# Strided and local attention with a dense mixture of attention experts: all weights loaded through one queue, and the planner's steps shifted by a table

## The chip, the cores and the metric

One Trainium2 chip, one of its cores. The metric is the device time of one execution in microseconds. TensorE (PE in the profile) multiplies matrices, VectorE (DVE), ScalarE (ACT) and GpSimd (POOL) work on rows of 128 partitions, SyncE (SP) issues transfers.

## The reference

Eight batches, eight heads, 576 positions, heads of 64. The first four heads see a window of 32 positions, the other four every 32nd position. The result, 512 wide, goes through four experts, each a causal attention of one head; a gate picks two experts per position.

```python
def _attn_ref(q, k, v):                      # 8, 8, 576, 64
    scores = scale * np.matmul(q, k.transpose(0, 1, 3, 2))
    mask_local = (rel >= 0) & (rel < stride)                 # stride 32
    mask_strided = (rel >= 0) & (pos[None, :] % stride == pos[:, None] % stride)
    masks = np.stack([mask_local if h < H // 2 else mask_strided for h in range(H)], axis=0)
    attn = softmax(np.where(masks, scores, -1e9))
    return np.matmul(attn, v)

def _moe_ref(x, w_gate, wq, wk, wv, wo):     # x: 8, 576, 512
    logits = x @ w_gate                      # top 2 of 4, softmax over the two
    for e in range(E):
        q, k, v = x @ wq[e], x @ wk[e], x @ wv[e]
        a = softmax(causal(scale * (q @ k.transpose(0, 2, 1))))
        ye = a @ v @ wo[e]
        out += (weight of e, where it is picked) * ye
```

## The kernel before

The kernel writes no instruction order by hand. Each step is put on a list by `op(eng, key, fn, ...)`: the engines that may run it with an assumed cost, a place on a time line (`key`), and the buffers it reads and writes. `schedule()` then plays the list through with these assumed costs: on each engine, of the steps that could start within 0.02 us of the earliest, the one with the smallest key is issued (`MODE_PEN` is added for TensorE where the shape of the rows and columns in use, the mode, would change). The order so found is the program; each engine executes its part strictly in order and waits by semaphores. A batch is `T = 52.0` wide on the time line.

`stage1(b, hp)` is the first attention of batch `b` for a pair of heads; pairs 0 and 1 are local, 2 and 3 strided. `load_qk` brings q and k into a tile `nat` (in batch 0, pairs 0 and 1 use tiles `p` of the later stage), TensorE transposes it (L422) into `qkt`, multiplies scores (L452), VectorE masks and takes maxima, GpSimd subtracts (L479), ScalarE exponentiates (L481), VectorE sums, GpSimd scales (L488), TensorE transposes the probabilities (L511, L513) into `pt` and multiplies with `v` (L537 local, L542 strided; this is called the values step). The result is kept as a sum of two reduced-precision parts, `xh` (ScalarE, L557) and `xl` (VectorE, L559). There are two tiles each of `nat`, `qkt`, `v` and `pt`, so the loads of a pair wait for the pair two before it.

`project` multiplies x with the weights of k and q (L651: 12 matmuls a group, four contraction tiles times three products of parts), `values2` those of v and the gate (L598). `attend(b, ep, ...)` does the causal attention for a pair of experts: scores (L704, L686), VectorE masks and takes the extreme (L715), ScalarE exponentiates (L722), GpSimd scales (L745, L739), TensorE transposes (L767) into `th` and multiplies with v (L803). `out_tile` multiplies with `wo` (L834) and stores.

`load_weights` brings a weight to a staging buffer and splits it, as x, into `wh` (ScalarE, L330) and `wl` (VectorE or GpSimd, L333). The staging of `wq`, `wk`, `wv` is already in the buffers `qk2` of the q and k of the second stage, that of `wo` in the buffers `ys` of the output. The load is one step for each 128 rows; `wk` and `wq` are issued by ScalarE, `wv` and `wo` by SyncE, and each waits until a given transposition of `stage1` has been issued in the planner's time line (`after=[behind]`).

Transfers of both issuing engines take eight semaphores in turn, and each waits until the transfer that last held its semaphore has landed.

## Time and profile before

| | us |
|---|---|
| median of 3 runs (lowest, highest) | 535.01 (530.88, 535.28) |
| the profiled execution | 533.24 |
| its span, first to last instruction | 531.5 |
| TensorE, VectorE, ScalarE, GpSimd busy | 500.9, 342.1, 298.7, 203.5 |

The profile is of one execution. A line number is that of the kernel; L251 is the copy out of the accumulators that all steps share. Busy time of TensorE is modelled from pipelined matmuls, so that a window that is full need not be at the engine's peak.

### The profile page before, as it was taken

The page shows a single profiled execution, that of the slowest core. Times are in us where ns is not written, and L with a number is a line of the kernel's source. Part 1 is how long each engine was busy: PE and PEld are TensorE (multiplying, and loading weights), DVE is VectorE, ACT ScalarE, POOL GpSimd, SP SyncE. Part 2 cuts the span into 40 slices and gives each one's busy share as a digit, 9 for nine tenths or more (in the row PEclk, how much of TensorE's full clock was granted, in tenths as well). Part 3 has the DMA queues.
Part 4 walks back from the last instruction along what each step waited for, and adds up shares of the span by engine and source line. Part 5 has one row for each costly group of instructions (what it writes and reads, how often), then busy time and mean ns, then how long its engine had stood idle before and what let it go on. Part 6 is the DMA issues. An engine that isn't in the chain of part 4 may idle for free.

```text
span 531.5 us, 17995 instructions
## 1 busy us (share of the span) xinstructions
PE 500.9 (94%) x7192; PEld 420.9 (79%) x7192; DVE 342.1 (64%) x1037; ACT 298.7 (56%) x829; POOL 203.5 (38%) x255
## 2 busy tenths in 40 slices
PE   4468999899999999999999999999999999999997
PEld 4458987788878887889878897789878888788864
DVE  4575488835676667865677666865778575833661
ACT  2263357743766556753666555754667555653652
POOL 6362226531544234341444243441344424520440
PEclk9965999999999999999999999999999999999999
DMA  7957333421344224541245214551245212110103
GB/s 141 175 128 160 81 87 70 107 53 24 77 118 114 58 45 109 133 100 25 61 117 130 57 29 105 140 114 26 46 130 133 47 25 65 41 42 1 41 20 100
DMA packets 138803, 43.53 MB, mean 82 GB/s; under 512 B 133856, under 2 KB 133856, under 8 KB 138720
## 3 DMA queue, kind: packets, MB, share of 16 engines
q1 hardware_dynamic: 134496, 41.34, 32.7%
q10 hardware_dynamic: 4224, 1.05, 1.0%
q8 instruction: 57, 0.93, 0.7%
q14 instruction: 26, 0.21, 0.1%
HBM read 32.92 MB, written 9.44 MB: 80 GB/s over the span
## 4 chain that ended last, share of the span: by engine, by line
PE 84%; DMA 4%; SPq 4%; DVE 3%; issue 2%; POOL 2%; ACT 1%; DVEq 0%; POOLq 0%; ACTq 0%
PE bank L651 21%; PE bank L598 11%; PE bank L834 10%; PE bank L803 9%; PE bank L704 8%; PE bank L767 6%; PE bank L452 5%; PE bank L542 4%; PE bank L537 3%; PE bank L422 3%; SPq L377 2%; DMA v<-in_v_dram 2%; PE bank L511 2%; PE bank L513 1%; SPq L371 1%
## 5 line engine op out<-in xcount | busy, mean ns | idle before, releaser
L745 POOL TENSOR_SCALAR p<-p,st,wt 128x192 f32<-128x192 f32 (+3 forms) x128 | 82.9, 662 | 69.6 <-ACT qkt L251 25.4
L722 ACT ACTIVATE p<-p,st 128x192 f32<-128x192 f32 (+3 forms) x128 | 78.3, 615 | 18.9 <-DVE st L715 18.2
L251 DVE COPY th<-bank 128x384 f32<-128x384 f32 (+2 forms) x92 | 42.4, 478 | 35.3 <-PE bank L767 30.9
L479 POOL TENSOR_TENSOR p1l<-p1l,st 128x960 f32<-128x960 f32 (+1 forms) x18 | 29.0, 1615 | 89.6 <-DVE st L477 72.9
L704 PE MATMUL bank<-qk 64*128 64x288 f32 (+3 forms) x320 | 59.2, 452 | 0.3 <-DVE pt L251 0.3
L251 ACT COPY qk<-bank 128x288 f32<-128x288 f32 x59 | 23.5, 398 | 63.2 <-PE bank L651 63.2
L715 DVE CUSTOM_DVE_ANT_0 p<-bank,m_cau 128x192 f32<-128x192 f32 (+3 forms) x128 | 57.1, 474 | 1.9 <-PE bank L704 1.4
L803 PE MATMUL bank<-th,vs 128*64 128x256 f32 (+1 forms) x512 | 57.0, 361 | 0.5 <-DVE th L251 0.4
L251 ACT COPY qkt<-bank 128x320 f32<-128x320 f32 (+3 forms) x93 | 32.9, 409 | 33.2 <-PE bank L422 24.0
L803 PEld LDWEIGHTS bank<-th,vs 128*64 128x64 f32 x512 | 35.1, 139 | 18.7 <-DVE p1s L466 1.3
L767 PEld LDWEIGHTS bank<-ident,p 64*128 64x128 f32 x896 | 38.4, 139 | 14.2 <-issue 8.0
L251 ACT COPY th<-bank 128x384 f32<-128x384 f32 (+2 forms) x100 | 40.5, 418 | 12.9 <-PE bank L767 7.4
L767 PE MATMUL bank<-ident,p 64*128 64x64 f32 x896 | 46.7, 228 | 0.2
L598 PE MATMUL bank<-wh_v,xh 128*128 128x260 f32 (+1 forms) x160 | 46.6, 291 | 0.3 <-ACT qkt L251 0.3
L488 POOL TENSOR_TENSOR p1l<-p1l,st 128x960 f32<-128x960 f32 (+1 forms) x18 | 29.0, 1614 | 46.6 <-DVE st L486 36.3
L479 POOL TENSOR_TENSOR p1s<-p1s,st 128x648 f32<-128x648 f32 (+1 forms) x18 | 20.7, 1154 | 67.3 <-DVE st L477 32.9
L598 PE MATMUL bank<-wl_v,xh 128*128 128x260 f32 (+1 forms) x160 | 45.3, 283 | 0.0
L598 PE MATMUL bank<-wh_v,xl 128*128 128x260 f32 (+1 forms) x160 | 45.0, 281 | 0.0
L452 PE MATMUL bank<-qkt 64*64 64x54 f32 (+1 forms) x1408 | 37.0, 247 | 7.2 <-ACT qkt L251 4.7
L651 PE MATMUL bank<-xh,wh_k 128*128 128x288 f32 x128 | 40.2, 314 | 0.7 <-ACT qkt L251 0.7
L452 PEld LDWEIGHTS bank<-qkt 64*64 64x64 f32 x1408 | 31.4, 144 | 11.1 <-ACT qkt L251 5.5
L559 DVE TENSOR_TENSOR xl<-bank,xh 128x320 fp32r<-128x320 f32 (+1 forms) x64 | 28.3, 454 | 18.2 <-ACT xh L557 17.9
(126 smaller groups left out, 1267.1 us busy)
## 6 DMA issues: line engine op xcount, KB each, us to landing
out_dram<-ys SPq DMA_DIRECT2D x32, 256.0 KB
v<-in_v_dram SPq DMA_DIRECT2D x32, 192.0 KB
v<-in_v_dram SPq DMA_DIRECT2D x96, 45.0 KB
nat<-in_q_dram SPq DMA_DIRECT2D x28, 144.0 KB
nat<-in_k_dram SPq DMA_DIRECT2D x28, 144.0 KB
nat<-in_q_dram SPq DMA_DIRECT2D x64, 49.5 KB
nat<-in_k_dram SPq DMA_DIRECT2D x64, 49.5 KB
nat<-in_q_dram SPq DMA_DIRECT2D x32, 45.0 KB
```

The source lines that it names most:

```text
L251: (nc.scalar.copy if e == "ACT" else nc.vector.tensor_copy)(dst, src)
L452: nc.tensor.matmul(sp[h].t[64 * hf:64 * hf + 64, nk * i:nk * i + nk], qkt.t[r, 0, q0:q0 + 64], qkt.t[r, 1, c0:c0 + nk], start=True, stop=True)
L479: nc.gpsimd.tensor_tensor(P, P, bc[0], ALU.subtract)
L598: nc.tensor.matmul(vp.t[:m, :NV], xx.t[:, t0:t0 + m], ww.t[:, kt, :], start=i == 0, stop=i == 11)
L651: nc.tensor.matmul(pj.t[:, :HS], ww.t[:, kt, ep * 128:(ep + 1) * 128], xx.t[:, c], start=i == 0, stop=i == 11)
L704: nc.tensor.matmul(sp[a].t[:, :cn], qk.t[r, 0, q0:q0 + m], qk.t[r, 1, c0:c0 + cn], start=True, stop=True)
L715: lambda e, sp=sp, p=p, a=a, c0=c0, cn=cn, hh=hh, nk=nk, acc_=acc_: nc.vector.tensor_tensor_reduce(out=p.t[:, a, c0:c0 + cn], in0=sp[a].t[ ...
L722: op({"ACT": 0.485 + 0.00083 * nk}, k_ + 1, lambda e, p=p, a=a, ci=ci: nc.scalar.activation(p.t[:, a], p.t[:, a], AF.Exp, bias=st.t[:, ci ...
L745: lambda e, p=p, a=a, ci=ci, t=t: nc.gpsimd.tensor_scalar(p.t[:, a], p.t[:, a], st.t[:, 14 + ci + a:15 + ci + a], wt.t[:, t, 2 * ep + a:2 ...
L767: nc.tensor.transpose(tp[hf].t[:, 64 * c:64 * c + 64], p2[t].t[r, a, k0:k0 + 128], ident[r, r])
L803: nc.tensor.matmul(acc.t[o, dst:dst + 128 * nb], vw, x.t[:, c:c + nb, :].rearrange("p c q -> p (c q)"), start=j == 0, stop=j == js[-1], sk ...
L834: nc.tensor.matmul(yp.t[:, :DM], xx.t[:, c0:c0 + 128], ww.t[:, ep, :], start=i == 0, stop=i == 5)
```

## The change

Three things. `load_weights` issues all weights from SyncE and no longer waits for a transposition; its places on the time line are new (`wk` 6.5 and `wq` 7.5 in place of -18 and -6.5, steps of 0.1 in place of 0.5). Every call of `op` gets a name, and a table `PRI` of 112 numbers is added to the key: one for the name, one more for the name in batch 0 and in batch 7. The planner starts VectorE, GpSimd and SyncE at 4.5, 9.0 and 0.8 in place of 0 and takes a packet of a transfer at 0.0014 in place of 0.0013. No step's function, tile or number of buffers changes.

```diff
+    batch = [0]
+
+    PRI = {
+        "acc": 1.0, "acc 0": 8.0, "acc 7": 2.0, "exp2": 1.0, "exp2 0": 10.0, "exp2 7": -4.0, "exp2_0": 15.0,
...
+        "yp_out": 18.0, "yp_out 0": -9.0, "yp_out 7": 10.0,
+    }
+
+    def op(kind, eng, key, fn, r=(), w=(), mode=None, npk=0, after=()):
...
-        o.eng, o.key, o.fn, o.mode, o.npk = eng, key, fn, mode, npk
+        o.eng, o.fn, o.mode, o.npk = eng, fn, mode, npk
+        o.key = key + PRI.get(kind, 0.0) + PRI.get(f"{kind} {batch[0]}", 0.0)
...
-        free = {e: 0.0 for e in LAT}
+        free = {"PE": 0.0, "ACT": 0.0, "DVE": 4.5, "POOL": 9.0, "SP": 0.8}
...
-                dma_free = max(dma_free, t) + o.npk * 0.0013
+                dma_free = max(dma_free, t) + o.npk * 0.0014
...
-    def load_weights(name, key, behind):
+    def load_weights(name, key):
...
-            k_ = key + 0.5 * kt
+            k_ = key + 0.1 * kt
...
-            op({"ACT" if name in "kq" else "SP": 0.55 + 0.4 * (name == "v")}, k_, load, w=[st], npk=512, after=[behind])
-            op({"ACT": act(n)}, 15 + k_ * 0.1, lambda e, kt=kt, raw=raw: nc.scalar.copy(hi.t[:, kt, :], raw()),
+            op("load_w", {"SP": 0.55 + 0.4 * (name == "v")}, k_, load, w=[st], npk=512)
+            op("hi_w", {"ACT": act(n)}, 15 + k_ * 0.1, lambda e, kt=kt, raw=raw: nc.scalar.copy(hi.t[:, kt, :], raw()),
...
-    for nm, key, hp in (("k", -18.0, 2), ("q", -6.5, 3), ("v", 12.5, 3), ("o", 14.5, 3)):
-        load_weights(nm, key, TPS[hp])
+    for nm, key in (("k", 6.5), ("q", 7.5), ("v", 12.5), ("o", 14.5)):
+        load_weights(nm, key)
```

What this does to the order is shown at three places. In the rows that follow, the numbers behind names tell buffers apart: `qkt_158` and `qkt_159` serve pairs 0 and 2, 1 and 3; `v_160` and `v_161` likewise; `nat_156` and `nat_157` serve pairs 2 and 3 in batch 0, then pairs 0 and 2, 1 and 3; `qk_143`, `qk_144`, `qk_145` stage `wk`, `wq`, `wv`. Lines of the changed kernel are 23 or 24 higher.

ScalarE in the opening, from the exponentials of pair 0 on, before:

```order
L481 ACTIVATE p1l_162<-p1l_162 128x480 x2
L251 COPY qkt_158<-bank_68 128x324
L324 DMA qk_143<-in_moe_wk_dram 128x4x64 x4
L251 COPY qkt_158<-bank_69 128x252
L251 COPY qkt_158<-bank_71 128x252
L330 CAST wh_k_222<-qk_143 128x256
```

and now:

```order
L504 ACTIVATE p1l_162<-p1l_162 128x480 x2
L275 COPY qkt_158<-bank_68 128x324
L275 COPY qkt_158<-bank_69 128x324
L275 COPY qkt_158<-bank_70 128x252
L275 COPY qkt_158<-bank_71 128x252
L504 ACTIVATE p1l_163<-p1l_163 128x480 x2
L275 COPY qkt_159<-bank_68 128x324
```

The issues of `wk` between the copies of pair 2 are gone, ScalarE makes all four copies itself, and the first cast of `wk` comes only behind pair 0's `xh`.

SyncE in the opening, from the last load of pair 1's `v` on, before:

```order
L401 DMA v_161<-in_v_dram 96x8x64
L324 DMA qk_145<-in_moe_wv_dram 128x4x64
L327 DMA qk_145<-in_moe_w_gate_dram 128x4
...
L322 DMA ys_140<-in_moe_wo_dram 128x512
L406 DMA v_160<-in_v_dram 18x10x64 x3
L409 DMA v_160<-in_v_dram 54x1x64
...
L322 DMA ys_141<-in_moe_wo_dram 128x512
L406 DMA v_161<-in_v_dram 18x10x64 x3
L409 DMA v_161<-in_v_dram 54x1x64
```

and now:

```order
L425 DMA v_161<-in_v_dram 96x8x64
L348 DMA qk_143<-in_moe_wk_dram 128x4x64 x4
L348 DMA qk_144<-in_moe_wq_dram 128x4x64
L430 DMA v_160<-in_v_dram 18x10x64 x3
L433 DMA v_160<-in_v_dram 54x1x64
...
L430 DMA v_161<-in_v_dram 18x10x64 x3
L433 DMA v_161<-in_v_dram 54x1x64
...
L348 DMA qk_144<-in_moe_wq_dram 128x4x64 x3
L348 DMA qk_145<-in_moe_wv_dram 128x4x64
L351 DMA qk_145<-in_moe_w_gate_dram 128x4
```

`wk` and a quarter of `wq` now go ahead of the `v` of pairs 2 and 3, the rest of `wq` and all of `wv` behind it.

SyncE at the loads for the strided pairs 2 and 3 of batch 2 (`nat_156`, then `nat_157`), before:

```order
L377 DMA nat_156<-in_q_dram 18x11x64 x2
L377 DMA nat_156<-in_q_dram 18x10x64
L398 DMA v_160<-in_v_dram 96x64
L401 DMA v_160<-in_v_dram 96x8x64
...
L377 DMA nat_156<-in_k_dram 18x11x64 x2
L377 DMA nat_156<-in_k_dram 18x10x64
L398 DMA v_161<-in_v_dram 96x64
```

and now:

```order
L401 DMA nat_156<-in_q_dram 18x11x64 x2
L401 DMA nat_156<-in_q_dram 18x10x64
L401 DMA nat_156<-in_k_dram 18x11x64 x2
L401 DMA nat_156<-in_k_dram 18x10x64
L422 DMA v_160<-in_v_dram 96x64
L425 DMA v_160<-in_v_dram 96x8x64
```

The `v` loads now stand behind the twelve of the tile. On TensorE the transpositions of this tile came right behind those of pair 1, one attention unit after pair 0's; now a block of 48 projection matmuls (L651) stands between the last transposition out of the buffer's earlier tile and the first out of this one.

## Rows read from the trace of the kernel before

**Rows 1.** The page: span; busy time, share and instructions of each engine; the chain that ended last by engine.

```profile
span 531.5 us, 17995 instructions
PE 500.9 (94%) x7192; PEld 420.9 (79%) x7192; DVE 342.1 (64%) x1037; ACT 298.7 (56%) x829; POOL 203.5 (38%) x255
...
PE 84%; DMA 4%; SPq 4%; DVE 3%; issue 2%; POOL 2%; ACT 1%; DVEq 0%; POOLq 0%; ACTq 0%
```

**Rows 2.** Windows: the stretch, its length, busy time and instructions of each engine in it, granted clock, share of the DMA engines, GB/s; and, from the time line of TensorE, its last matmul (start, duration).

```profile
0.00:49.04 49.04, 28.44 (x498) 25.37 (x499) 29.67 (x68) 20.41 (x52) 27.01 (x47) 0.80 0.72 147
49.04:108.08 59.04, 56.65 (x889) 48.73 (x887) 40.33 (x124) 33.42 (x98) 24.47 (x28) 0.93 0.44 96
108.08:167.19 59.11, 58.98 (x878) 49.32 (x877) 38.12 (x121) 35.92 (x100) 19.61 (x23) 1.00 0.31 76
...
470.55:531.50 60.95, 56.57 (x496) 44.21 (x495) 24.27 (x94) 27.70 (x80) 14.37 (x23) 1.00 0.12 40
...
527.41 0.40 PE L834 MATMUL bank<-wl_o,oh 128*128 128x512 f32 x1
```

**Rows 3.** Time line of ScalarE in the opening: start, duration, instruction, and in brackets the idle time before it with what ended it.

```profile
21.49 0.64 ACT L251 COPY qkt<-bank 128x252 f32<-128x252 f32 x2 [6.57 <-DMA qk<-in_moe_wk_dram]
...
29.21 0.75 ACT L251 COPY pt<-bank 96x320 f32<-96x320 f32 x2 [4.37 <-DMA qk<-in_moe_wq_dram]
```

**Rows 4.** Time line of TensorE in the opening, same columns.

```profile
21.91 1.59 PE L452 MATMUL bank<-qkt 64*64 64x54 f32 x44 [4.32 <-ACT qkt L251]
...
24.63 1.28 PE L511 MATMUL bank<-ident,p1l 64*96 64x64 f32 x20
...
29.68 2.18 PE L537 MATMUL bank<-pt,v 96*64 96x64 f32 x34 [3.37 <-ACT pt L251]
...
35.20 2.18 PE L537 MATMUL bank<-pt,v 96*64 96x64 f32 x34 [0.18 <-ACT pt L251]
...
45.32 2.64 PE L542 MATMUL bank<-pt,v 54*64 54x54 f32 x44 [1.93 <-DVE pt L251]
47.89 1.22 PE L422 MATMUL bank<-ident,nat 64*128 64x64 f32 x18
49.04 0.61 PE L651 MATMUL bank<-xh,wh_k 128*128 128x288 f32 x1
```

**Rows 5.** Time line of GpSimd in the opening, same columns.

```profile
18.57 1.93 POOL L488 TENSOR_TENSOR p1l<-p1l,st 128x480 f32<-128x480 f32 x2
...
27.17 1.42 POOL L479 TENSOR_TENSOR p1s<-p1s,st 128x324 f32<-128x324 f32 x2 [3.13 <-DVE st L477]
...
33.02 1.41 POOL L333 TENSOR_TENSOR wl_k<-qk,wh_k 128x256 fp32r<-128x256 f32 x2 [2.54 <-ACT wh_k L330]
...
36.54 1.78 POOL L488 TENSOR_TENSOR p1s<-p1s,st 128x324 f32<-128x324 f32 x2
```

**Rows 6.** Time line of SyncE's queue in the opening: the issues of `wv` with the gate, first and last, and of pair 2's `v`, first and last.

```profile
22.30 0.54 SPq L324 DMA_DIRECT2D qk<-in_moe_wv_dram  x1
...
25.96 1.61 SPq L327 DMA_DIRECT2D qk<-in_moe_w_gate_dram  x1
...
31.05 1.09 SPq L406 DMA_DIRECT2D v<-in_v_dram  x3
...
34.40 0.75 SPq L409 DMA_DIRECT2D v<-in_v_dram  x1
```

**Rows 7.** Time lines of SyncE's queue and of TensorE at two places where transpositions of q and k wait for their tile.

```profile
100.76 1.27 SPq L377 DMA_DIRECT2D nat<-in_k_dram  x3
...
221.26 1.09 SPq L377 DMA_DIRECT2D nat<-in_q_dram  x3
...
225.88 1.16 SPq L377 DMA_DIRECT2D nat<-in_k_dram  x3
...
104.68 0.85 PE L422 MATMUL bank<-ident,nat 54*128 54x54 f32 x11 [1.39 <-DMA nat<-in_k_dram]
...
229.12 0.55 PE L422 MATMUL bank<-ident,nat 54*128 54x54 f32 x11 [0.88 <-DMA v<-in_v_dram]
```

**Rows 8.** The chain that ended last, in order of time: start, duration up to the next piece, piece.

```profile
49.11 5.31 PE bank L651 x24
...
55.40 3.38 PE bank L651 x24
...
108.08 4.96 PE bank L651 x36
...
113.56 1.79 PE bank L651 x12
...
155.68 1.41 PE bank L542 x44
```

**Rows 9.** The waits of TensorE from 49 to 475 us: waiting line, what ended the wait, us in total, times, longest.

```profile
PE bank L422 <- DMA v<-in_v_dram: 1.7, 2, 0.9
PE bank L422 <- DMA nat<-in_k_dram: 1.4, 1, 1.4
...
PE bank L422 <- DMA nat<-in_q_dram: 0.2, 1, 0.2
```

**Rows 10.** Windows of the opening, columns as in the second group.

```profile
15.00:20.00 5.00, 0.46 (x4) 0.32 (x4) 2.90 (x7) 0.00 (x0) 3.33 (x4) 1.00 0.74 168
...
30.00:35.00 5.00, 5.00 (x104) 4.43 (x100) 3.01 (x7) 3.55 (x11) 1.89 (x3) 0.50 0.40 91
```

More of the change, by code (lines that the diff above doesn't have):

```diff
@@ L347, in attention_moe_kernel @@
     X = {}
-    TPS = []
     def stage1(b, hp):
+        batch[0] = b
         h0 = 2 * hp
@@ L424, in tps @@
                     c += w_
-            first = op({"PE": 0.058 * len(ws) + 0.03}, k0 - 14 + u, tps, r=[nat], w=[*tp, qkt], mode=MR)
+            op("tp", {"PE": 0.058 * len(ws) + 0.03}, k0 - 14 + u, tps, r=[nat], w=[*tp, qkt], mode=MR)
             for x in range(2):
-                op(either(cn), k0 - 13 + u, lambda e, t_=tp[x], x=x, c0=c0, cn=cn: copy(
+                op("tp_out", either(cn), k0 - 13 + u, lambda e, t_=tp[x], x=x, c0=c0, cn=cn: copy(
                     e, qkt.t[:, x, c0:c0 + cn], t_.t[:, :cn]), r=[tp[x]], w=[qkt])
         for h in range(2):
-            op({"SP": 1.0 if local else 1.9}, (k0 - 25 if b else 4.0 + hp), lambda e, h=h: load_v(e, h), w=[vt], npk=864 if local else 594)
-        TPS.append(first)
+            op("load_v", {"SP": 1.0 if local else 1.9}, (k0 - 25 if b else 4.0 + hp), lambda e, h=h: load_v(e, h), w=[vt], npk=864 if local else 594)
         sp = [RB.new(f"s{h}_{n}") for h in range(2)]
@@ L453, in scores @@
                                          qkt.t[r, 0, q0:q0 + 64], qkt.t[r, 1, c0:c0 + nk], start=True, stop=True)
-        op({"PE": 1.0 if local else 0.75}, k0 - 11, scores, r=[qkt], w=[*sp, p[0], p[1]], mode=MQ)
+        op("s", {"PE": 1.0 if local else 0.75}, k0 - 11, scores, r=[qkt], w=[*sp, p[0], p[1]], mode=MQ)
         N = 2 * ni * nk
@@ L499, in stage1 @@
                 r_, w_ = ((ph, sh), (ph + sh, ph), (ph, ph), (ph, sh), (sh, sh), (ph + sh, ph))[step]
-                op(eng, k0 - 9 + step, lambda e, step=step, h_=h_: softmax(step, h_, e), r=r_, w=w_)
+                op(f"softmax{step}", eng, k0 - 9 + step, lambda e, step=step, h_=h_: softmax(step, h_, e), r=r_, w=w_)
         ptt = PTR.new(f"pt_{n}")
@@ L521, in stage1 @@
                 rows = 96 if local else 128
-                op(either(64 * ni), k0 - 1.5 + 0.5 * u, lambda e, pt=pt, hf=hf, dst=dst, rows=rows: copy(
+                op("pt_out", either(64 * ni), k0 - 1.5 + 0.5 * u, lambda e, pt=pt, hf=hf, dst=dst, rows=rows: copy(
                     e, dst(), pt[hf].t[:rows, :64 * ni]), r=[pt[hf]], w=[ptt])
@@ L555, in xv @@
                 return t.rearrange("c (j r) -> c j r", r=STR)[:, :, c0 // NJ:(c0 + cn) // NJ]
-            op({"ACT": act(cn)}, k0 + 0.5 + 0.3 * u, lambda e, s_=sv_, xv=xv: nc.scalar.copy(xv(xh.t), s_()),
+            op("xh", {"ACT": act(cn)}, k0 + 0.5 + 0.3 * u, lambda e, s_=sv_, xv=xv: nc.scalar.copy(xv(xh.t), s_()),
                r=[xa], w=[xh[u]])
-            op({"DVE": dve(cn)}, k0 + 1 + 0.3 * u, lambda e, s_=sv_, xv=xv: nc.vector.tensor_sub(
+            op("xl", {"DVE": dve(cn)}, k0 + 1 + 0.3 * u, lambda e, s_=sv_, xv=xv: nc.vector.tensor_sub(
                 xv(xl.t), s_(), xv(f(xh.t))), r=[xa, xh[u]], w=[xl[u]])
@@ L599, in mm @@
                         i += 1
-            op({"PE": 12 * 0.121}, key + step * t, mm, r=xbufs(b) + wbufs("v"), w=[vp, vs[t]], mode=M128)
-            op(either(NV), key + step * t + 0.5, lambda e, t=t, m=m, vp=vp: copy(e, vs.t[:m, t, :], vp.t[:m, :NV]),
+            op("vp", {"PE": 12 * 0.121}, key + step * t, mm, r=xbufs(b) + wbufs("v"), w=[vp, vs[t]], mode=M128)
+            op("vp_out", either(NV), key + step * t + 0.5, lambda e, t=t, m=m, vp=vp: copy(e, vs.t[:m, t, :], vp.t[:m, :NV]),
                r=[vp], w=[vs[t]])
@@ L653, in mm @@
                         i += 1
-            op({"PE": 12 * 0.134}, key + step * u, mm, r=xbufs(b) + wbufs(nm), w=[pj, qk[j, u]], mode=M128)
-            op(either(HS), key + step * u + 0.5, lambda e, u=u, pj=pj: copy(
+            op("pj", {"PE": 12 * 0.134}, key + step * u, mm, r=xbufs(b) + wbufs(nm), w=[pj, qk[j, u]], mode=M128)
+            op("pj_out", either(HS), key + step * u + 0.5, lambda e, u=u, pj=pj: copy(
                 e, qk.t[:, j, u * HS:(u + 1) * HS], pj.t[:, :HS]), r=[pj], w=[qk[j, u]])
@@ L731, in attend @@
         kk = key + 3.6 * (len(idx) - 1) + 1.5
[L732 removed]
+        op("recip2", {"DVE": 0.4}, kk, recip, r=[st["s"]], w=[st["r"]])
         for t in idx:
@@ L858, in attention_moe_kernel @@
         k2 = T * (b + 0.75) + 3
+        batch[0] = b
         qk = [QK2.new(f"qk_{b}_{ep}") for ep in range(2)]
```

56 lines of the change are left out of this document (28 added, 28 removed), and 15 rows, old and new, of the table PRI.

## The prediction

> **What bounds the kernel now.** I read the page first: TensorE is busy 94% of the span, and the chain of work that ended last runs over it for 84% [rows 1]. Next the windows cut the span into stages, since that share is an average over stages with different limits [rows 2]. Before 49.04 us TensorE is busy for 28.44 us only; from 49.04 to 108.08 us it misses 2.39 us, in the next 59 us 0.13 us. So there are two regimes: an opening of 49 us in which TensorE waits, and some 480 us in which it is the bound and only its own work counts. The end adds little: the last window misses 4.38 us, of which 3.69 are the last copy and store behind the last matmul (527.81 us) [rows 2].
>
> The opening decides most, so I read it engine by engine. ScalarE stands still for 6.57 us in front of two copies at 21.49 us, with the four issues of `wk` ahead of them in its queue, and for 4.37 us in front of the copies at 29.21 us, behind the issues of `wq` [rows 3]. TensorE waits for exactly these copies: 4.32 us for the scores of pair 2 (21.91 us) and 3.37 us for the values step of pair 0 (29.68 us) [rows 4]. The issues take long because each waits for an earlier transfer to land; ScalarE, in program order, then cannot copy.
>
> **The change: the opening.** Three edits act together. The eight loads of `wk` and `wq` leave ScalarE for SyncE, `load_weights` no longer waits for a transposition, and the offsets in PRI rearrange what is ready. The order shows ScalarE's copies of pair 2 in one row with no transfer between them, and no weight transfer on ScalarE at all. So both waits go: 4.32 + 3.37 = 7.69 us. What is late next?
>
> First GpSimd: the probabilities of pair 0 are scaled from 18.57 us for 1.93 us [rows 5], so their transpositions cannot start before 20.50 us, where before they started at 24.63 us [rows 4]. That step moves by 4.1 us, not 4.3. Pair 1's values step ended at 35.20 + 2.18 = 37.38 us [rows 4]; without both waits it ends at 37.38 - 7.69 = 29.7 us. GpSimd's work for all four pairs from 20.50 us on, as the new order has it: 1.42 + 1.93 + 1.42 + 1.78 + 1.78 for the softmax and 4 x 0.71 for three pieces of `wl_k` and one of `wl_q` [rows 5], 11.2 us, hence 31.7 us, some 33 us with two waits of half a microsecond for scores. It stays just ahead of TensorE.
>
> Then SyncE. Pair 3's `v` goes into the buffer that pair 1's values step frees, so its eight issues start at 29.7 us and take 4.1 us (31.05 to 35.15 us before [rows 6]): 33.8 us. A load lands 2.1 to 2.6 us after its last issue: 225.88 + 1.16 = 227.04 us against transpositions at 229.12 us, and 100.76 + 1.27 = 102.03 us against 104.68 us [rows 7]. So pair 3's values step starts at 36.2 us; it takes 2.64 us, and 1.1 us (a cast and a subtraction) lie between its end, 47.96 us, and the first projection, 49.04 us [rows 4]. First projection after: 36.2 + 2.64 + 1.1 = 39.9 us, 9.1 us earlier. The 18 transpositions of batch 1 that stood ahead of it (1.15 us [rows 4]) now come behind: net **-8.0 us**. Bounds: if the steps run at the full clock from pair 1 on, 37.4 us, net -10.5; if landing through one queue costs another 3.6 us, 43.5 us, net -4.4. I take the middle, since every row in it is a wait seen in this opening.
>
> Do the weights arrive in time, last in SyncE's queue? The three remaining `wq` loads issue until 35.3 us (0.5 each), `wv` with the gate takes 5.3 us more (22.30 to 27.57 us [rows 6]), to 40.6 us. `wq` lands at 37.9 us and needs some 1.5 us of casting; TensorE asks for it after 24 `k` matmuls, 39.9 + 5.31 = 45.2 us [rows 8]. `wv` lands at 43.2 us and is split by 45.2 us; it is asked for at 45.2 + 3.38 = 48.6 us. Batch 1's first tile follows `wv` on the queue (2.8 us of issues) and lands at 46.0 us, asked for at 48.6 us. So this costs nothing while SyncE runs less than 2.6 us late; beyond that TensorE waits by as much.
>
> Here a rule speaks against the change. The row: issuing from ScalarE blocked 6.57 and 4.37 us of it and cost TensorE 7.69 us [rows 3, 4]. The Trainium skill, "DMA: Bandwidth & Descriptors", section "Issuing engines are not separate DMA queues", says that transfers from all issuing engines share the same DMA engines, and that a second issuer saves only the sequencer's issue time, usually small beside the transfer. By that alone the move gains no bandwidth and adds eight issues of about half a microsecond to SyncE, +4 us where SyncE is late; by the rows it gains 7.69 us. The rows decide, as what is expensive here is what the issue keeps waiting behind it.
>
> **The change: modes of TensorE.** A group of 12 projection matmuls costs 1.79 us, one of 36 costs 4.96 us [rows 8]: 12 matmuls more cost 1.585 us, so 0.20 us of each group is neither, and I put 0.10 us on each of its two edges, where matmuls of another row and column shape stand. Counting such edges along TensorE's whole queue in both orders gives 268 before and 244 after. 24 x 0.10 = **-2.4 us**. Bounds 0 (hidden where TensorE waits anyway) to -3.
>
> **The change: transpositions that waited for their tile.** After 49 us TensorE's largest waits are in L422, 1.7 and 1.4 us in three places, and a last 0.2 [rows 9]. At 227 us the strided tile of pair 2 is asked for some 7 us after its buffer was freed: SyncE starts its 12 loads at 221.26 us and they land at 229.12 us [rows 7]; at 104.68 us four `v` loads even stand between its loads. In the new order 48 projection matmuls (6.5 us) and some ten other steps stand between the two uses, in every batch, and the `v` loads follow the tile's own. All three waits go: 1.7 + 1.4 + 0.2 = **-3.3 us**. Bounds 0 (another load takes the place) to -3.3.
>
> **The change: everything else moved.** The offsets shift nearly every step by up to 20 on a scale on which a batch is 52. With ScalarE at 56% and VectorE at 64% there is room, but steps issued in order can wait. Below: the other idle time after 49 us, about 1.7 us, goes. Above: one new wait like the 1.39 us of [rows 7] in four batches, +5.6 us. I take 0, the row to which 0.13 us in 59 us [rows 2] is nearest. Renaming, the planner's other starting times and its dearer transfers (0.0014 for 0.0013) issue nothing of their own.
>
> **Sum.** -8.0 - 2.4 - 3.3 = -13.7 us. The profiled execution took 533.24 us, 1.74 more than its span, and lies between the runs (530.88 to 535.28, median 535.01). 533.24 - 13.7 = **519.5 us**, -2.9% on the median.
>
> **Rivals.**
> *The clock stays up.* From 15 to 20 us the granted clock was 1.00 (2.4 GHz), with TensorE busy for 0.46 us of five; from 30 to 35 us it was 0.50 (1.2 GHz) [rows 10]. It came back only in the projections, whose first 24 matmuls took 5.31 instead of 3.38 us [rows 8]. Without the two long waits TensorE may keep 2.4 GHz: 1.9 us there and 1.2 us in pair 3's values step (2.64 us; 44 such matmuls later take 1.41 at the full clock [rows 8]), with some of pair 1's: 519.5 - 4 = 515.5, and 513 with the short waits gone. For it: the denser opening. Against it: from 30 to 35 us TensorE was busy all five microseconds at half clock [rows 10], and after 30 us it will still wait for GpSimd and SyncE. The Trainium skill, "TensorE: Matmul & The Clock Gate", section "Why this matters for your kernels", advises to keep TensorE continuously busy and without gaps between bursts to get and hold the full clock. By that the opening would run at 2.4 GHz; no row at the new density exists.
>
> *The opening alone pays.* New in-order waits eat what modes and tiles give, or SyncE is the bound it can be: 533.24 - 8.0 + 3 = 528, or with a first projection at 43.5 us and the rest as forecast 523. For it: all loads in one queue, with waits for TensorE between them.
>
> *Slower.* GpSimd executes in order, and the new table puts scalings of probabilities (L745) behind softmax steps of the next batch whose input may come late; TensorE's transpositions L767 wait for the scalings. There are 14 such units in batches 1 to 7 (two pairs of experts each). If each waits 1.4 us, the largest wait of this kind on TensorE [rows 7], that is 19.6 us: 539. It decides from 1.0 us per unit on. Against it: GpSimd is busy 38% [rows 1], and before, with the same queue, no wait for GpSimd shows in TensorE's list from 49 to 475 us [rows 9].
>
> *It doesn't do what it says.* Staging weights in the q/k buffers is in the kernel before already, so that part of the description moves nothing; if GpSimd's chain, not ScalarE, held the opening, the time stays within 1%, 530 to 537.
>
> **How the numbers follow.** Forecast (516 to 523) 0.50; clock stays up (511 to 516) 0.20; opening alone (523 to 529) 0.19; no change 0.07; slower 0.04. The range 512 to 528 leaves out the last two, the far end of the clock rival and little of the third. A measurement of this kernel can tell about 1% from no change: faster is below 529.7. Faster 0.89, same 0.07, slower 0.04.
>
> **What would show it.** Right: no wait of ScalarE for a weight transfer before 40 us; first projection near 40 us; pair 3's values step released by a load of `v`; no idle time in front of the transpositions of q and k after the first projection; the windows of a batch as full as before. A first projection after 44 us breaks the first term; TensorE idle in front of the second transpositions, released by GpSimd, means the slower rival. Most likely to be wrong is the size of the first term: three engines come within 3 us of each other there.

## The result and the profile after

The changed kernel takes **509.49 us** (median of 4 runs, 508.14 to 511.71) against 534.41 us of the kernel before (4 runs beside it, 530.88 to 535.28): a ratio of 0.955, 95% interval 0.949 to 0.961. The forecast was 519.5 with 512 to 528: the sign was right, the size too small, and the time lies outside the range.

The profiled execution took 508.14 us, its span 506.4, 25.1 us less than before. First the page, its lines as in [rows 1]:

```profile
span 506.4 us, 17970 instructions
PE 487.6 (96%) x7192; PEld 411.9 (81%) x7192; DVE 342.0 (68%) x1033; ACT 298.5 (59%) x831; POOL 205.5 (41%) x257
...
PE 88%; SPq 4%; DVE 2%; DMA 2%; ACT 1%; issue 1%; POOL 1%; POOLq 0%; ACTq 0%; DVEq 0%
```

TensorE does the same 7192 matmuls and is shown as busy for 487.6 us instead of 500.9. This is the first thing that the sum didn't foresee: it took TensorE's own time for nearly fixed. Where the 25.1 us lie is read from windows cut at TensorE's first projection, at that of batch 1 and at that of batch 7 (columns as in [rows 2]). Before:

```profile
0.00:49.04 49.04, 28.44 (x498) 25.37 (x499) 29.67 (x68) 20.41 (x52) 27.01 (x47) 0.80 0.72 147
49.04:108.01 58.97, 56.58 (x889) 48.66 (x887) 40.33 (x124) 33.42 (x98) 24.40 (x28) 0.93 0.43 96
108.01:470.39 362.38, 359.16 (x5315) 302.48 (x5314) 247.82 (x752) 216.99 (x601) 137.68 (x158) 1.00 0.32 78
470.39:531.48 61.09, 56.73 (x497) 44.37 (x495) 24.27 (x94) 27.86 (x80) 14.37 (x23) 1.00 0.12 40
```

and after:

```profile
0.00:37.03 37.03, 24.41 (x480) 21.20 (x480) 23.08 (x59) 17.93 (x45) 23.93 (x45) 0.80 0.68 139
37.03:92.65 55.62, 54.50 (x894) 46.96 (x892) 42.39 (x124) 37.11 (x105) 25.28 (x28) 0.98 0.59 126
92.65:445.83 353.18, 352.52 (x5321) 298.66 (x5319) 253.09 (x760) 214.95 (x600) 143.28 (x165) 1.00 0.34 82
445.83:506.36 60.53, 56.22 (x504) 45.09 (x502) 23.44 (x92) 28.52 (x82) 12.96 (x21) 1.00 0.12 40
```

The opening gives 12.0 us, the first batch 3.4, the six batches after it 9.2, the end 0.6. Some 1.0 of the 9.2 us is work that the new order moves over the window's edges: the traces show one output tile less (six matmuls) and twelve transpositions more in it. So there are two questions: why the first projection comes at 37.0 and not at 39.9 us, and where the 13.1 us behind it come from, of which the sum had 4.55 (-2.4 - 3.3 + 1.15).

The opening on TensorE's time line, the lines that answer to [rows 4]:

```profile
20.49 0.77 PE L534 MATMUL bank<-ident,p1l 64*96 64x64 f32 x10 [0.18 <-POOL p1l L511]
...
26.02 1.63 PE L560 MATMUL bank<-pt,v 96*64 96x64 f32 x36 [0.23 <-ACT pt L275]
28.84 0.90 PE L536 MATMUL bank<-ident,p1s 64*128 64x64 f32 x12 [1.18 <-POOL p1s L511]
...
34.47 2.63 PE L565 MATMUL bank<-pt,v 54*64 54x54 f32 x44 [0.61 <-ACT pt L275]
37.03 0.61 PE L674 MATMUL bank<-xh,wh_k 128*128 128x288 f32 x1
```

The two waits of [rows 4] behind ScalarE's copies (4.32 and 3.37 us) are gone. The second transpositions start at 20.49 us, where the prediction had 20.5, released by GpSimd as it said. Pair 1's values step ends at 27.65 (forecast 29.7), and the last one runs straight into the first projection. SyncE carries all weights, and with them is late for one thing that TensorE asks for, batch 1's first tile behind the weights:

```profile
45.49 0.74 PE L446 MATMUL bank<-ident,nat 64*128 64x64 f32 x17 [0.69 <-DMA nat<-in_k_dram]
```

Its queue (start, duration, issue, count):

```profile
21.36 2.19 SPq L348 DMA_DIRECT2D qk<-in_moe_wk_dram  x4
...
30.59 1.53 SPq L430 DMA_DIRECT2D v<-in_v_dram  x3
32.16 0.73 SPq L433 DMA_DIRECT2D v<-in_v_dram  x1
32.94 1.54 SPq L348 DMA_DIRECT2D qk<-in_moe_wq_dram  x3
```

And TensorE's waits from 49 to 475 us, where [rows 9] had three lines of transpositions waiting for their tile:

```profile
PE bank L857 <- ACT th L275: 0.5, 2, 0.3
PE bank L446 <- DMA nat<-in_k_dram: 0.3, 1, 0.3
```

### The profile page after: what moved, and what is told of

It reads as the page before. It is cut to its first block, busy times and chain, and to the rows that moved or that the text cites. A ratio compares the mean times of both kernels' runs of the same rounds, so it can differ in the third digit from the quotient of the medians.

```text
span 506.4 us, 17970 instructions
## 1 busy us (share of the span) xinstructions
PE 487.6 (96%) x7192; PEld 411.9 (81%) x7192; DVE 342.0 (68%) x1033; ACT 298.5 (59%) x831; POOL 205.5 (41%) x257
## 4 chain that ended last, share of the span: by engine, by line
PE 88%; SPq 4%; DVE 2%; DMA 2%; ACT 1%; issue 1%; POOL 1%; POOLq 0%; ACTq 0%; DVEq 0%
PE bank L674 20%; PE bank L621 11%; PE bank L857 11%; PE bank L826 10%; PE bank L727 9%; PE bank L790 6%; PE bank L475 5%; PE bank L565 4%; PE bank L446 4%; PE bank L560 4%; PE bank L534 2%; SPq L395 1%; PE bank L709 1%; DMA nat<-in_k_dram 1%; PE bank L536 1%
## 5 line engine op out<-in xcount | busy, mean ns | idle before, releaser
L275 DVE COPY th<-bank 128x384 f32<-128x384 f32 (+2 forms) x87 | 40.0, 476 | 41.1 <-PE bank L790 30.5
L738 DVE CUSTOM_DVE_ANT_0 p<-bank,m_cau 128x192 f32<-128x192 f32 (+3 forms) x128 | 56.2, 476 | 11.5 <-PE bank L727 10.5
L826 PE MATMUL bank<-th,vs 128*64 128x256 f32 (+1 forms) x512 | 55.3, 356 | 0.0
L727 PE MATMUL bank<-qk 64*128 64x288 f32 (+3 forms) x320 | 54.9, 444 | 0.0
L790 PEld LDWEIGHTS bank<-ident,p 64*128 64x128 f32 x896 | 37.0, 139 | 14.1 <-issue 5.5
L275 ACT COPY qkt<-bank 128x252 f32<-128x252 f32 (+3 forms) x106 | 37.3, 409 | 12.1 <-PE bank L446 12.1
L275 ACT COPY qk<-bank 128x288 f32<-128x288 f32 x46 | 18.3, 398 | 44.1 <-PE bank L674 43.8
L674 PE MATMUL bank<-xh,wh_q 128*128 128x288 f32 x128 | 38.5, 301 | 0.0
L674 PE MATMUL bank<-xl,wh_k 128*128 128x288 f32 x128 | 38.0, 297 | 0.0
L674 PE MATMUL bank<-xh,wl_k 128*128 128x288 f32 x128 | 38.0, 297 | 0.0
L674 PE MATMUL bank<-xh,wl_q 128*128 128x288 f32 x128 | 37.7, 294 | 0.0
```

The lines of the kernel that those rows point to most:

```text
L275: (nc.scalar.copy if e == "ACT" else nc.vector.tensor_copy)(dst, src)
L674: nc.tensor.matmul(pj.t[:, :HS], ww.t[:, kt, ep * 128:(ep + 1) * 128], xx.t[:, c], start=i == 0, stop=i == 11)
L727: nc.tensor.matmul(sp[a].t[:, :cn], qk.t[r, 0, q0:q0 + m], qk.t[r, 1, c0:c0 + cn], start=True, stop=True)
L738: lambda e, sp=sp, p=p, a=a, c0=c0, cn=cn, hh=hh, nk=nk, acc_=acc_: nc.vector.tensor_tensor_reduce(out=p.t[:, a, c0:c0 + cn], in0=sp[a].t[ ...
L790: nc.tensor.transpose(tp[hf].t[:, 64 * c:64 * c + 64], p2[t].t[r, a, k0:k0 + 128], ident[r, r])
L826: nc.tensor.matmul(acc.t[o, dst:dst + 128 * nb], vw, x.t[:, c:c + nb, :].rearrange("p c q -> p (c q)"), start=j == 0, stop=j == js[-1], sk ...
```

## The experiments

Three theories. **A**: the opening is gained by taking `wk` and `wq` off ScalarE, the rest by the table in the later batches. **B**: the opening needs the table too. **C**: the later gain follows from the earlier opening. Within A, what the table does later: tiles that arrive in time (A1), changes of mode, or waits of TensorE inside stretches that the profile shows as busy. All windows are those of the section above; "six batches" is from the first projection of batch 1 to that of batch 7.

### One half of the change at a time

`e1_loads`, the kernel before with the new loads alone:

```diff
-            op({"ACT" if name in "kq" else "SP": ...}, k_, load, w=[st], npk=512, after=[behind])
+            op({"SP": 0.55 + 0.4 * (name == "v")}, k_, load, w=[st], npk=512)
...
-    for nm, key, hp in (("k", -18.0, 2), ("q", -6.5, 3), ("v", 12.5, 3), ("o", 14.5, 3)):
+    for nm, key in (("k", 6.5), ("q", 7.5), ("v", 12.5), ("o", 14.5)):
```

> The kernel before with the weight loads of the change alone: all issued by SyncE, no wait for a transposition, the new places on the time line; no table, and the planner's starting times and transfer cost as before. Theory A (the opening is gained by taking wk and wq off ScalarE, everything later by the table): the two waits of 4.32 and 3.37 us are gone, the first projection comes near 37 to 38 us instead of 49.0, and from there on the stretches cost what they cost before (59 us to the first projection of batch 1, 362 us for six batches): 521 to 523 us. Rival B (the opening needs the offsets of batch 0 too): the first projection is not before 43 us, 527 us or more. Rival C (what came after the first projection follows from the earlier opening, since the loads of all later batches then run further ahead): the later stretches shrink by some 13 us here too, 508 to 511 us.

Measured: 533.0 us, ratio 0.998 (0.994 to 1.002): **no gain at all**, and none of the three theories holds (B's time would fit, its late opening doesn't). The windows tell why (from the first projection on):

```profile
37.45:95.48 58.03, 54.83 (x894) 46.91 (x893) 45.12 (x131) 35.36 (x100) 21.90 (x25) 0.98 0.63 121
95.48:469.44 373.96, 363.50 (x5323) 304.21 (x5319) 244.25 (x750) 217.37 (x606) 141.26 (x162) 0.99 0.32 77
```

The first projection comes at 37.45 us, 11.6 us earlier, just as A has it. But the six batches take 374.0 us instead of 362.4: the gain is given back in full. TensorE's waits in the six batches:

```profile
PE bank L772 <- POOL p L739: 3.0, 2, 2.0
PE bank L422 <- DMA nat<-in_k_dram: 2.3, 3, 0.9
PE bank L452 <- DVE qkt L251: 1.1, 2, 0.5
PE bank L513 <- POOL p1s L488: 1.0, 2, 0.6
```

The first line is the mechanism of the rival called *Slower*: transpositions of the experts wait for GpSimd's scaling. On GpSimd itself:

```profile
128.62 0.45 POOL L739 TENSOR_SCALAR p<-p,st,wt 128x128 f32<-128x128 f32 x1 [3.43 <-DMA wt<-wt]
```

The scaling waits 3.43 us for the small transfer of the gate's weights (issued at 124.75 us), which in this order comes late in two of the six batches (67.2 and 66.3 us each, the others 58 to 61). Waits for GpSimd are 4.0 of the 10.5 us that TensorE idles in the six batches (3.2 before). In the same two batches a run of short waits is followed by a stretch at the lower level of TensorE's clock (0.50, which is 1.2 GHz; windows, columns as in [rows 2]; then a step that begins ahead of the second window and ends in it):

```profile
153.80:158.80 5.00, 2.59 (x67) 2.19 (x64) 4.01 (x11) 3.08 (x8) 2.17 (x2) 1.00 0.56 126
158.80:162.20 3.40, 3.40 (x48) 2.76 (x46) 1.32 (x3) 1.68 (x5) 3.40 (x5) 0.50 0.56 127
...
158.35 2.23 PE L542 MATMUL bank<-pt,v 54*64 54x54 f32 x44
```

The same 44 matmuls take 1.41 us at the full level [rows 8]. In the two batches the steps L542 and L803 that lie there take some 3.0 us more in all than at the full level. So 7.2 of the 11.6 us lost are idle time, and most of the rest is the clock. An earlier opening moves every later step against the others in the planner's play, and the order that comes out has its own waits.

`e2_table`, the changed kernel with the old loads (the reverse of the diff above):

> The changed kernel with the weight loads of the kernel before (wk and wq issued by ScalarE, each behind a given transposition, old places on the time line); the table and the planner's new starting times stay. Theory A: ScalarE again stands behind its issues, the first projection comes at 46 to 50 us; from there on it is as in the changed kernel (55.6 us to the first projection of batch 1, 353 us for six batches): 519 to 523 us. Rival C (the gain after the first projection follows from the earlier opening): the stretches after it are as before, 59 and 362 us, 531 to 535 us.

Measured: 535.0 us, ratio 1.005 (1.001 to 1.008), so each half alone is worth nothing and the two together 25 us. The opening is A's: ScalarE's waits are back, and TensorE has them:

```profile
21.73 1.59 PE L477 MATMUL bank<-qkt 64*64 64x54 f32 x44 [4.32 <-ACT qkt L275]
...
29.80 0.68 PE L477 MATMUL bank<-qkt 64*64 64x54 f32 x12 [4.08 <-ACT qkt L275]
```

The first projection is at 48.46 us. The later part is neither A's 353 nor C's 362, but 367.2 us: the table doesn't carry its gain over to another opening. Here too a part is the clock: from 282.0 to 292.2 us the granted clock is 0.50.

`e4_b0_only` keeps the loads and the table in batch 0, `e5_no_table` the loads and the planner's starting times without any table:

```diff
-        o.key = key + PRI.get(kind, 0.0) + PRI.get(f"{kind} {batch[0]}", 0.0)
+        o.key = key + ((PRI.get(kind, 0.0) + PRI.get(f"{kind} {batch[0]}", 0.0)) if batch[0] == 0 else 0.0)
```

(`e5_no_table` has `o.key = key`.)

> The changed kernel with the table's numbers used in batch 0 only; all later batches keep their old places on the time line. Theory A: opening as in the changed kernel (37 us), later stretches nearly as before (362 us for six batches, a few us less at most): 518 to 523 us. Rival C: 508 to 511 us.

> The changed kernel with the table's numbers all left out; new weight loads and the planner's new starting times and transfer cost stay. Theory A: as with the loads alone, 37 to 38 us at the first projection and 521 to 523 us. Rival D (the planner's starting times and its dearer transfers, which the prediction put at nothing, give a part of the gain after the opening): the six batches take clearly less than the 362 us of before, 512 to 518 us.

Measured: 519.97 and 523.37 us, one run each. First projection at 36.61 and 38.93 us, six batches 362.1 and 364.0 us. So A holds for the opening (B falls: the loads without the table bring it to 37 to 39 us; D falls with the 364.0 us), and C falls for the rest: with an opening as early as that of the changed kernel the six batches are as long as before. `e5_no_table` and `e1_loads` differ only in the planner's starting times and its price of a transfer, which issue nothing; yet the six batches differ by 10 us, through the order (some 3.0 of them by the clock in `e1_loads`).

### Which numbers of the table

```diff
-        o.key = key + PRI.get(kind, 0.0) + PRI.get(f"{kind} {batch[0]}", 0.0)
+        o.key = key + (PRI.get(kind, 0.0) + PRI.get(f"{kind} {batch[0]}", 0.0) if batch[0] == 0 or kind in ("load_qk", "load_v") else 0.0)
```

This is `e8_b0_loads`. In place of its last condition `e7_no_loadshift` has `kind not in ("load_qk", "load_v")`, `e9_b0_pe` `"PE" in eng` and `e10_no_pe` `"PE" not in eng`.

> The changed kernel, but in batches 1 to 7 the loads of q, k and v keep their old places on the time line; all other numbers of the table stay. The six stretches from the first projection of batch 1 to that of batch 7 took 362.4 us before and 353.2 us in the changed kernel. Theory A1 (transpositions that wait for their tile, as the prediction sized them): the waits for the tile come back in this kernel, 2.5 to 3.3 us, so 356 us. Theory A2 (the order on TensorE and the steps that feed it give the gain, not the loads): 353 to 354.5 us. Rival (the table works only as a whole, since each number was found with all the others in place): 360 us or more.

> The changed kernel with the whole table in batch 0, but in batches 1 to 7 only the loads of q, k and v are shifted. Theory A1: 359 us for the six stretches (362.1 us with nothing shifted there, less the 3 us of waits for the tile). Theory A2: 362 us. Rival (only as a whole): 362 us or more, here not told apart from A2.

> The changed kernel with the whole table in batch 0; in batches 1 to 7 only TensorE's own steps are shifted (transpositions, scores, values, projections, output), all steps of the other engines and the loads keep their places. Theory A2 in its first form (TensorE's own order gives the gain, by fewer changes of mode): 355 to 357 us for the six stretches. In its second form (the steps that feed TensorE do, because TensorE waits inside stretches in which it is shown busy): 360 to 362 us.

> The counterpart: the whole table in batch 0; in batches 1 to 7 all steps but TensorE's own are shifted. Its order has 283 changes of mode, against 244 of the changed kernel and 268 of before. First form (changes of mode): 362 us or more for the six stretches. Second form (the feeding steps): 355 to 358 us.

Measured (one run each: 524.36, 523.52, 515.95 and 524.13 us), with the lines of the six batches; in the table "changes" are those of the mode that the steps declare to the planner, counted in the order. Counted by the rows and columns that the traces show (up to 64 or more) they are 188, 190, 208, 199, 203, 191 and 178.

| numbers used in batches 1 to 7 | six batches, us | TensorE idle, us | changes |
|---|---|---|---|
| (kernel before) | 362.4 | 3.2 | 193 |
| none | 362.1 | 3.4 | 195 |
| loads | 367.1 | 4.9 | 208 |
| all but loads | 366.0 | 5.2 | 199 |
| all but TensorE's | 365.5 | 4.3 | 207 |
| TensorE's | 356.7 | 0.6 | 194 |
| all | 353.2 | 0.7 | 176 |

```profile
96.42:453.14 356.72, 356.14 (x5309) 300.64 (x5307) 246.71 (x743) 218.97 (x610) 141.23 (x162) 1.00 0.33 80
```

This line is `e9_b0_pe`. A1 falls as a theory of separate gains: shifting only the loads costs 5.0 us against none, leaving out only the loads 12.9 against all. Both fit the rival that the table works only as a whole. The 12.9 us are not the waits for tiles alone: 4.5 of them are idle time, of whatever cause, and behind two runs of waits the clock falls again, the longer time so:

```profile
270.10:280.30 10.20, 9.10 (x109) 7.88 (x110) 6.25 (x15) 4.82 (x13) 4.83 (x6) 0.50 0.67 150
```

TensorE's own numbers give 5.4 of 8.9 us, in the range that was named for the first form, but not for its reason: the changes of mode are 194, as before. What went, against no numbers at all (`e4_b0_only`), is 2.8 us of idle time and 2.5 us of time shown as busy (358.7 to 356.1), with the same number of changes. But the windows don't hold the same work: `e9_b0_pe` has one output tile (some 1.4 us) and twelve transpositions (some 0.5 us) less in them than `e4_b0_only`, so 1.9 of the 2.5 us are work at the edges. With work counted alike, TensorE's numbers give some 3.5 of 7.5 us.

### What a change of mode costs

```diff
                         i += 1
+                        if i in (4, 8):
+                            nc.tensor.matmul(pj.t[:, 320:384], W[nm][0].t[0:64, 0, 0:128], X[b, 0][0].t[0:64, 0:64],
+                                             start=True, stop=True, skip_group_check=True)
```

The counterpart has `0:128` for `0:64` of the rows.

> The changed kernel with two small extra matmuls inside each group of 12 projection matmuls (128 in all, 64 columns each, into unused columns of the same accumulator, results not used), on 64 rows: TensorE changes its mode to them and back, 256 changes more. Nothing else moves. Its counterpart has the same extra matmuls on 128 rows, without a change. If a change costs the 0.10 us that the prediction took, this one is 25.6 us slower than the counterpart; if 0.12 us, as the times between matmuls of the traces give, 31 us; if the price of [rows 8] is mostly something else, less than 13 us.

> The counterpart: the same 128 extra matmuls on 128 rows, with no change of mode. Against the changed kernel only their own columns come in: 64 of 288 columns of a projection matmul that takes 0.132 us, so some 0.03 to 0.06 us each, 4 to 8 us in all: 513 to 517 us.

Measured: spans of 567.4 and 520.1 us. The whole difference, 47.3 us, has an opening in it that ran at the other clock level; the six batches, at 1.00 in both, are cleaner, on 64 rows and on 128:

```profile
106.26:500.01 393.75, 393.10 (x5416) 319.78 (x5414) 251.59 (x760) 214.66 (x600) 142.85 (x165) 1.00 0.30 74
93.95:457.80 363.85, 363.19 (x5416) 309.31 (x5414) 252.50 (x760) 214.86 (x600) 143.22 (x165) 1.00 0.33 79
```

29.9 us for 192 changes: **0.156 us a change**, not the 0.10 of the sum. On the time line of the first one, the extra matmul between two projection matmuls that otherwise follow each other in 0.13 us:

```profile
179.59 0.29 PE L674 MATMUL bank<-xl,wh_q 128*128 128x288 f32 x1
179.82 0.29 PE L678 MATMUL bank<-xh,wh_q 64*128 64x64 f32 x1
180.04 0.40 PE L674 MATMUL bank<-xh,wl_q 128*128 128x288 f32 x1
```

No idle time is shown at a change: it lies in durations and starts. The Trainium skill, "TensorEngine Tiling (Array Packing)", section "Key Properties", says that a change of the tiling mode drains TensorE; these runs agree and give the price for changes between 128 and 64 rows inside a group. The extra matmul on 128 rows cost 0.11 us (10.7 us for 96 in the six batches), twice what was expected of it.

### What TensorE waits for while it is shown as busy

```diff
+    class Short:
...
+            if cur[0] < 2 or name == "dma_start":
+                return fn
+            return lambda *a, **k: fn(*[cut(x) for x in a], **{n: cut(x) for n, x in k.items()})
+
+    vec_, sca_, gps_ = Short(nc.vector), Short(nc.scalar), Short(nc.gpsimd)
```

All calls of the three engines go through these; `cut` leaves 8 columns. TensorE's order is that of the original, matmul by matmul.

> The kernel before, in its own order, but from batch 2 on VectorE, ScalarE and GpSimd work on only 8 columns of each row (results not used), except for the two steps that split the experts' output; TensorE's matmuls and all transfers are whole. From the first projection of batch 3 to that of batch 7 the kernel before took 240.8 us and the changed one 234.5 us. Theory H (TensorE waits for the feeding engines inside stretches that the profile shows as busy): 234 us or less here, some 6 us below its own 240.8, although only about 2 us of idle time are shown. Rival M (the matmuls themselves take longer in the old order, by changes of mode and shapes): within 2.5 us of 240.8.

> The changed kernel with the same shortening. Theory H: 233 us or a little less from the first projection of batch 3 to that of batch 7, since hardly a wait is left in it: no more than 2 us below its own 234.5, and within 2 us of the shortened kernel before, the rest being 17 changes of mode in six batches. Rival M: as far below the shortened kernel before as the changed one is below the kernel before, 6 us.

Measured, from the first projection of batch 3 to that of batch 7: before and shortened, then after and shortened.

```profile
229.60:470.39 240.79, 238.91 (x3518) 201.15 (x3516) 164.83 (x502) 143.23 (x396) 92.60 (x107) 1.00 0.31 76
226.85:464.74 237.89, 236.80 (x3517) 199.54 (x3515) 71.50 (x502) 66.46 (x397) 33.69 (x105) 1.00 0.31 77
```

```profile
211.35:445.83 234.48, 234.07 (x3525) 198.50 (x3521) 169.18 (x509) 141.79 (x395) 96.03 (x111) 1.00 0.32 78
209.83:443.40 233.57, 233.57 (x3524) 198.11 (x3521) 71.82 (x508) 66.25 (x395) 35.68 (x111) 1.00 0.32 78
```

Both theories missed; the truth lies between. Feeding engines cost the kernel before 2.9 us in these four batches and the changed one 0.9, so 2.0 of the 6.3 us between them. Of the 2.9, 2.1 were shown as **busy** time of TensorE (238.91 to 236.80). One group shows it, 12 transpositions in the kernel before and the same ones in its shortened form:

```profile
282.85 0.96 PE L513 MATMUL bank<-ident,p1s 64*128 64x64 f32 x12
```

```profile
279.78 0.54 PE L537 MATMUL bank<-ident,p1s 64*128 64x64 f32 x12
```

Nothing stands in brackets at the first, and 0.42 us of it are a wait. The Trainium skill, "Perfetto Trace Analysis", section "Summary: the profiler window per engine type", says that the profiler's end of a TensorE instruction is an estimate; the trace agrees in that a full window is no proof. The other 4.3 us of the 6.3: the tile's wait that stays in the shortened kernel before (1.1 us idle), ten declared changes of mode fewer (127 to 117, 1.6 us; by the shapes in the traces only five, 0.8 us), one output tile that the new order moves across the window's edge less twelve transpositions that it moves in (some 1.0 us), and 0.6 to 1.4 us without an owner.

### Does the clock hold the opening?

Extra small matmuls in TensorE's waits of the opening are meant to change its clock and nothing else:

```diff
+    def warm(bank, n, c=384):
+        for _ in range(n):
+            nc.tensor.matmul(bank.t[:, c:512], ident, ident[:, 0:512 - c], start=True, stop=True, skip_group_check=True)
+
+    WARM = {("tp", 0, 0): 10, ("tp", 0, 1): 1, ("s", 1): 1, ("tp", 2, 1): 2, ("s", 2): 1, ("tp", 3, 1): 2, ("pt", 2, 0): 3, ("xa", 2): 2, ("xa", 3): 2}
...
+                        if b == 0 and g == 0:
+                            warm(tp[0], WARM.get(("tp", hp, x), 0))
```

> The changed kernel with 32 small matmuls (ident with 32 columns of itself, into unused columns of an accumulator, results not used) ahead of TensorE's first transposition, where it waits 5.96 us for its first tile. Nothing else moves. The rival on the clock said that the opening would keep 2.4 GHz by itself; it didn't (the values steps of pairs 2 and 3 took 2.63 us each, 1.41 at the full clock, and the first 24 projection matmuls 4.18 instead of 3.38). If work ahead of the first tile is enough to keep the clock up to the first projection, that comes at 33 to 35 us instead of 37.03 and the projection takes 3.38: 504 to 507 us. If the gaps between 11 and 20 us let it fall again: 508 to 510 us, with the first steps alone faster.

> The same with two to eight such matmuls more in each wait of 0.4 us or more of the opening (pairs 0 to 3), 41 in all. If the clock is what the opening lost, the values steps of pairs 2 and 3 take 1.41 us instead of 2.63 and the first 24 projection matmuls 3.38 us: first projection at 33 to 35 us, 503 to 506 us. If GpSimd's chain ends last there whatever TensorE's clock, the first projection stays within 1 us of 37.0 and only the 0.8 us of the projections is gained: 507 to 509 us. If the added matmuls hold up the steps behind them: 510 us or more.

These two missed their purpose: one such matmul took 0.43 us (64 instructions, 13.86 us), so the opening itself came 8.5 and 12.5 us later (518.71 and 525.85 us). Cut to the gaps:

> As warm_start, with the extra matmuls cut to the gap: 10 of 128 columns ahead of TensorE's first transposition, at 0.43 us each as measured there 4.3 us of the 5.96 us that it waits for its first tile. Results not used, nothing else moves. If work ahead of the first tile keeps the clock up: first projection at 33 to 35 us instead of 37.03. If not (in warm_start 13.9 us of such work did not: the scores behind it still took 1.90 and 2.10 us): 36.5 to 37.5 us, 508 to 511 us in all.

> As warm_gaps, with the extra matmuls cut to the gaps: 10 ahead of the first tile and 14 in the waits of the opening, one to three each. In warm_gaps the values steps of pairs 0 and 1 ran at the full clock (1.27 us for 36 matmuls, 2.19 in the changed kernel). If TensorE's clock held the opening: those of pairs 2 and 3 at 1.41 us and the first projection at 33 to 35 us, 503 to 506 us. If GpSimd's chain and the copies hold it: first projection within 1 us of 37.0, 507 to 510 us.

Measured: 507.59 us (one run) and 511.63 us (ratio 0.9615, 0.958 to 0.965). First projection at 36.15 and 36.48 us. `warm2_gaps` from pair 2's values step on:

```profile
29.02 1.54 PE L579 MATMUL bank<-pt,v 54*64 54x54 f32 x44
31.41 0.59 PE L548 MATMUL bank<-ident,p1s 64*128 64x64 f32 x12 [0.84 <-POOL p1s L521]
...
34.02 2.53 PE L579 MATMUL bank<-pt,v 54*64 54x54 f32 x42 [1.10 <-DMA v<-in_v_dram]
36.48 0.61 PE L688 MATMUL bank<-xh,wh_k 128*128 128x288 f32 x1
```

Pair 2's step takes 1.54 us instead of 2.63, and the 1.1 us won turn into waits at once: for GpSimd's scaling (0.84) and for pair 3's `v` (1.10), the two ends that the first term was worked out from. So up to pair 2's step the chain holds the opening, not the clock. Behind it the test doesn't reach: pair 3's 42 matmuls took 2.53 us, the first 24 projection matmuls 5.17 us, and the granted clock is 0.50 from 35 to 40 us. What the full level would give there isn't shown. Neither run beats the changed kernel by more than runs differ: 507.59 lies just below its 508.14 to 511.71, 511.63 within it.

## Why the prediction was right and wrong

**What bounds the kernel.** The two regimes held, and so did the sign. The sentence that failed is that in the second regime "only its own work counts", read off windows in which TensorE misses 0.13 us of 59 [rows 2]. With it failed the term "everything else moved", which was put at nothing: behind the first projection 13.1 us went, where the sum had 4.55.

**Opening** (-9.1 at the first projection; measured -12.0). Right: the two waits go, GpSimd's start at 20.5 us, nothing late on SyncE ahead of the first projection, and the cause (the loads alone bring 11.6). Two terms of its chain were too long. The "cast and a subtraction" of 1.1 us between the last values step and the first projection were the 18 transpositions of batch 1 (47.89 us, 1.22 us long [rows 4]): counted in the chain, and once more as work that moves behind. In the changed kernel the step ends at 37.10 and the projection starts at 37.03. And pair 3's values step starts at 34.47 instead of 36.2: pair 1's ended 2 us earlier than forecast, taking 1.63 us where [rows 4] has 2.18, and `v` of pair 3 was issued from 28.54 us on instead of 29.7, right behind pair 2's. The step is not released by `v`, as foreseen, but by ScalarE's copy of its own transpositions, for which TensorE waits 0.61 us. The rule weighed against the change (the Trainium skill, "DMA: Bandwidth & Descriptors", "Issuing engines are not separate DMA queues") would have put SyncE 4 us late; in the changed kernel the first five of the eight issues were through at 24.10 us, before pair 2's `v` was issued at 24.21 us, and the first projection waited for none of the eight.

**Modes** (-2.4). The count of 24 goes by the modes that the steps declare; by the rows and columns that the traces show the changes are 265 and 246, 19 fewer. The price was 0.156 us and not 0.10: -3.0 to -3.7 as an estimate, at or outside the bound of -3. It was measured for one kind of change only. [rows 8] could only give a price with part of the group's own work in it.

**Tiles** (-3.3). The three waits are gone; new ones of 0.7 and 0.3 us take their place (the first at 45.49 us, in batch 1's first tile), so -2.3. That the shift of the loads alone would do it is wrong: alone it costs 5 us.

**Everything else** (0, bounds -1.7 to +5.6). This is the term that broke the range: the lower bound was the idle time shown, and waits inside busy stretches are not in it. Behind the first projection 13.1 us went. Of them: modes 2.8 to 3.6 (one change of the count lies in the opening); tiles 2.3; the first 24 projection matmuls took 4.18 us instead of 5.31 [rows 8], 1.1 (37.03 to 41.21 us), since the full clock came back sooner behind the first projection; the feeding engines' waits 2.0 in four batches, some 3.5 in seven as an estimate from that; less 0.7 for the 18 transpositions that now come behind. That makes 9.0 to 9.8 of 13.1; **3.3 to 4.1 us are not settled by any run**. That the planner's starting times "issue nothing of their own" was true and no reason: through the order they are worth 10 us where there is no table. What they are worth beside the table wasn't tried.

**Rivals.** *Clock stays up* named the nearest time (513), but its mechanism happened in part only: the granted clock fell to 0.85 from 15 to 20 us and 0.50 from 20 to 25, came back for pair 1's values step (1.63 instead of 2.18 us) and fell again, and raising it up to pair 2 leaves the first projection within 1 us. Its ground, the 1.00 from 15 to 20 us in [rows 10], was no record of the clock (see the last section). *Slower* gave the right mechanism for the wrong kernel: waits for GpSimd's scaling appear when the loads are moved without the table, as 4.0 us of the 11.6 that are lost; in the changed kernel they are 0.5 us in one place. *The opening alone pays* (528 or 523) is what `e4_b0_only` and `e5_no_table` do, at 520 and 523.

## What to carry to other kernels

A window in which the bounding engine is shown as busy throughout can still hold waits: compare the same group of instructions in its shortest and longest occurrence before taking its idle time as a lower bound of what a reordering can give. Where a planner sets the order, an edit that frees an opening moves everything behind it, so its gain is read stage by stage, not from the total: here either half of the change was worth 0, both together 25 us. A run of short waits can cost twice, once as idle time and once more as matmuls at the lower level of the clock behind it (`e1_loads`, 2.23 us for a step of 1.41). Before adding a step that was moved to a chain, look whether it already is the gap that the chain was read from.

## What the runs showed of the hardware

A granted clock of 1.00 in a window can mean that the trace has no entry of the clock there: the view counts such a stretch as full. In `e5_no_table` the first entry stands at 40.70 us, so the windows read 1.00 in the whole opening, yet pair 3's values step takes as long as where the changed kernel's record reads 0.50 (window, then step):

```profile
35.00:40.00 5.00, 4.38 (x60) 4.12 (x61) 2.32 (x5) 2.32 (x6) 0.74 (x1) 1.00 0.60 126
```

```profile
36.36 2.64 PE L565 MATMUL bank<-pt,v 54*64 54x54 f32 x44 [0.62 <-ACT pt L275]
```

At the full clock the same 44 matmuls take 1.41 us [rows 8], and up to the first entry projection matmuls follow each other in 0.24 us, behind it in 0.13. In the kernel before the first entry stands at 26.05 us; 40 matmuls of scores took 1.91 us at 8.01 us, 1.05 later at the full level. In the changed kernel, too, the spacing changes where the entry of the full clock stands, at 39.0 us. The duration of a known step tells the level where the view may not.

A small f32 matmul on all 128 rows cost nearly the same with 32 columns as with 128 at the start of these runs: 0.217 us an instruction with 32 columns (13.86 us for 64), 0.232 with 128 (4.64 us for 20), and each such matmul is two instructions. In `warm_start` the scores behind 13.86 us of them without a gap took 1.90 and 2.10 us, as long as in the slow parts of the other openings; the first entry of the clock stands at 34.87 us there.
